# Down projection of a gated feed-forward block by a 2x2 seven-product scheme, with transposed output and sums kept on chip

## The chip, the cores and the metric

One Trainium2 chip, one NeuronCore. The metric is device time in microseconds (us) of one execution. The kernel before was run three times and profiled once.

## The reference

All data are float32. `x` is 2048 tokens by D = 512. Branch A is linear attention with 32 heads of width 16, branch B a bilinear feed-forward block with F = 1792; a sigmoid gate per token mixes them.

```python
g = sigmoid((x * gate_w).sum(-1, keepdims=True))
qkv = x @ wqkv                                   # 512 -> 3*512, 32 heads of 16
phi = lambda t: where(t > 0, t + 1, exp(t)) + 1e-6
kv = einsum("bhsd,bhse->bhde", phi(k), v); z = phi(k) summed over s
a = (phi(q) @ kv / (phi(q) @ z + 1e-6)) @ wo
b = ((x @ w_gate) * (x @ w_up)) @ w_down
out = g * a + (1 - g) * b
```

## The kernel before, in words

Every product of full precision is made of three TensorE matmuls (`mm3`): both operands are split into a high part (rounded to float32r, on ScalarE) and a low part (the difference, on VectorE), and high*high, low*high and high*low are summed in PSUM. TensorE takes a 128x128 block as stationary operand and 512 columns as moving operand.

Stage 1 (up to about 94 us of the profile) computes phi(k) for all tokens and the 512x512 matrix phi(k)^T x (`gt`), the column sums `zacc`, and the gates `gcol` (g) and `ocol` (1-g), one column of 16 token tiles each. `kv_unit` and `wp_unit` then fold the value weights and `wo` into one matrix (`wp`, four blocks of 128 rows) that is applied to phi(q).

Stage 2 goes twice (pair 0, pair 1) over two chunks of 512 tokens (c = 0, 1). A pass has 16 units: 14 "f" units, each 128 columns of `w_gate` and `w_up`, and two "q" units, each 256 columns of the query weights, after f units 5 and 9. A unit computes its 2x2 block product (two chunks by two column blocks) by the Winograd form of Strassen's scheme: seven products, into four PSUM banks Y, X, R, S (`unit`, `product`), each of six matmuls. The weights of a unit come as a load of five blocks (`w_load`), a negated copy of two of them on ScalarE and an accumulating DMA from GpSimd (`w_add`), and are split by `w_high` and `w_low`. The seven combinations of x per pair (`xc`) are parked in DRAM for pair 1 as high and low parts (`xpark`).

The hidden values `hh`, `hl` of two f units are multiplied by two rows of blocks of `w_down` (`dh`, `dl`) in eight jobs of one 128-token tile each (`down_jobs`): stationary are 128 tokens of the hidden values, moving 512 columns of `w_down`, six matmuls a job. A job ends with a scaled accumulation into its tile's sum `acc` by VectorE (`scalar_tensor_tensor` with `ocol`). The phi(q) part goes through the same jobs, with `gcol` and the folded matrix, which lies in DRAM meanwhile (`wpark`) and is loaded again for each q unit. `shares` says how many jobs stand at four places within a unit. Output tiles are tokens by D.

Every engine executes its instructions in the order in which the program writes them. A DMA of the SyncE (SP) queue also waits until the one eight places ahead of it, whose completion semaphore it uses again, has landed.

Of the kernel before, what the change touches and what calls it, by code (L numbers as in the profile page):

```python
# [31 lines left out]
NH = 5  # L32

SLOT = {3: 0, 4: 1, 5: 2, 2: 3, 1: 4, 6: 5, 7: 6}  # L40


@with_exitstack
def gated_mix(ctx: ExitStack, tc, xt, xp, x, wqkv, wq, wq_add, wo, wgu, wgu_add, wdn, gate_w, out):
# [74 lines left out]
    xpark = {i: [dram.tile([P, 2, CH], F32, name=f"xpark{i}{v}") for v in "hl"] for i in range(1, 8)}  # L119
    wpark = [[dram.tile([P, D], F32, name=f"wpark{b}{v}") for v in "hl"] for b in range(KT)]  # L120


    order = []
    for f in range(NF):
        order.append(("f", f))
        if f in (5, 9):
            order.append(("q", f // 9))
# [22 lines left out]
    def w_high(n):  # L150
        if n < len(order):
            wcs[n] = [const.tile([P, 7, 2 * P], F32R, tag=f"wc{v}", name=f"wc{v}", bufs=2) for v in "hl"]
            for a, b in PARTS:
                act(wcs[n][0][:, a:b], raws[n][:, a:b])
# [14 lines left out]
    def x_add(tile_, pair, i, ks):  # L169
# [3 lines left out]
        if one is not None:  # L173
# [3 lines left out]
    accs = [psum.tile([P, D], F32, tag=tag, name=f"gt{d}", bufs=2)  # L177
            for d, tag in enumerate(("att", "att", "dn", "dn"))]
    with tc.tile_pool(name="p1", bufs=2, reuse_waits="tile") as p1:
# [167 lines left out]
        pin(nc.vector.tensor_scalar(ocol, gcol, -1.0, 1.0, op0=ALU.mult, op1=ALU.add))  # L347
        pz = psum.tile([P, D], F32, tag="X", name="pz")
# [11 lines left out]
    jobs, at = [], {}  # L360

    def later(n, place, fn):
        at.setdefault((n, place), []).append(fn)

    def do(n, place):
        for fn in at.pop((n, place), []):
            fn()

    def down(k):
        for fn in jobs[:k]:  # L370
            fn()
        del jobs[:k]

    shares = {2: (0, 1, 1, 1), 6: (1, 0, 1, 0), 7: (1, 0, 1, 0), 10: (1, 1, 1, 2), 11: (1, 2, 1, 2),
              12: (1, 1, 1, 2), 15: (1, 1, 1, 2)}
    early = {units: (2, 3, 1, 2), units + 1: (2, 2, 2, 2)}

    def share(n):
        return early.get(n) or shares.get(n % units, (1, 1, 1, 1))

    def unit(n, quad):

        wh, wl = wcs.pop(n)
        bank = {t: psum.tile([P, CH], F32, tag=t, name=f"b{t}") for t in "YXRS"}

        def reload(i):
            if n + 1 == units:  # L390
                for src, part in zip(xpark[i], xc[i]):
                    dma(part.bitcast(F32), src)

        def product(i, to, start=False):
            for k in range(2):
                ks = slice(k * P, (k + 1) * P)
                mm3(bank[to], (wh[:, SLOT[i], ks], wl[:, SLOT[i], ks]), [v[:, k] for v in xc[i]],
                    start and k == 0, k == 1, not start)
            reload(i)

        m2 = p2.tile([P, CH], F32, tag="t", name="m2")
        cross = p2.tile([P, 2, CH], F32, tag="cross", name="cross")
        product(2, "Y", True)
        act(m2, bank["Y"])
        product(3, "X", True)

        tt(bank["R"], bank["X"], m2, ALU.subtract)
        do(n, "e")
        many = share(n)
        down(many[0])  # L410
        product(4, "Y")
        act(cross[:, 0], bank["Y"])
        do(n, "m")
        do(n, "c")
        down(many[1])
        do(n, "d")
        w_add(n + 2)
        product(1, "R")
        t = p2.tile([P, CH], F32, tag="t", name="t")
        tt(t, bank["R"], cross[:, 0], ALU.add)  # L420
        if n:
            w_high(n + 1)
        do(n, "t")
        product(5, "X")
        tt(bank["S"], t, bank["X"], ALU.subtract)
        act(cross[:, 1], bank["X"])
        if n:
            w_low(n + 1, 0)
        down(many[2])
        if quad:  # L430
            quad(1, 0, cross[:, 0])
        if n:
            w_low(n + 1, 1)
        do(n, "s")
        down(many[3])
        w_low(n + 1, 2)
        w_load(n + 3)
        if quad:
            quad(0, 1, cross[:, 1])
        product(6, "R")  # L440
        if quad:
            quad(1, 1, bank["R"])
        else:
            hh, hl = hidden()
            tt(cross[:, 1], bank["R"], cross[:, 1], ALU.mult)
            act(hh[:, 1], cross[:, 1])
        do(n, "r")
        product(7, "S")
        if quad:
            quad(0, 0, bank["S"])  # L450
        else:
            tt(cross[:, 0], bank["S"], cross[:, 0], ALU.mult)
            act(hh[:, 0], cross[:, 0])

            for c in 1, 0:
                def low(c=c):
                    tt(hl[:, c], cross[:, c], hh[:, c].bitcast(F32), ALU.subtract)

                if n + 1 == len(order):
                    later(n, f"low{c}", low)  # L460
                else:
                    low()
            return hh, hl

    def hidden():
        return [p2.tile([P, 2, CH], F32R, tag=f"h{v}", name=f"h{v}", bufs=NH) for v in "hl"]

    def down_tiles():
        return [p2.tile([P, D], F32R, tag=f"d{v}", name=f"d{v}", bufs=NH) for v in "hl"]

# [3 lines left out]
    def wp_load():  # L474
        att["wv"] = [p2.tile([P, D], F32, tag="acc", name="wv", bufs=8) for _ in range(KT)]
        att["wo"] = [p2.tile([P, D], F32, tag="ph", name="wo_sb", bufs=4) for _ in range(KT)]
        for k in range(KT):
            dma(att["wv"][k], wqkv[k * P:(k + 1) * P, 2 * D:3 * D])
        for k in range(KT):
            dma(att["wo"][k], wo[k * P:(k + 1) * P, :])  # L480

    def g_evac():
        att["g"] = [p2.tile([P, D], F32, tag="acc", name="gts", bufs=8) for _ in range(KT)]
        for d in range(KT):
            if d % 2:
                act(att["g"][d], accs[d])
            else:
                pin(nc.vector.tensor_copy(att["g"][d], accs[d]))

    def kv_unit():  # L490
        pkv = psum.tile([P, KT, P], F32, tag="att", name="pkv", bufs=2)
        for b in range(KT):
            sl = slice(b * P, (b + 1) * P)
            for d in range(KT):
                mm(pkv[:, b], att["wv"][d][:, sl], att["g"][d][:, sl], start=d == 0, stop=d == KT - 1)
        att["pkv"] = pkv

    def kv_split():
        kvm = p2.tile([P, KT, P], F32, tag="z", name="kvm", bufs=4)
        tt(kvm, att["pkv"], bmask[:, None, :].to_broadcast([P, KT, P]), ALU.mult)  # L500
        att["kvm"] = [p2.tile([P, KT, P], F32R, tag="z", name=f"kvm{v}", bufs=4) for v in "hl"]
        split(*att["kvm"], kvm)

    def wo_split(b):
        if b % 2 == 0:
            att.setdefault("woh", []).append(hidden())
        split(*[v[:, b % 2] for v in att["woh"][b // 2]], att["wo"][b])

    def wp_unit(b):
        pw = psum.tile([P, D], F32, tag="att", name="pw", bufs=2)  # L510
        mm3(pw, [v[:, b] for v in att["kvm"]], [v[:, b % 2] for v in att["woh"][b // 2]], True, True)
        d = down_tiles()
        split(*d, pw)
        for there, part in zip(wpark[b], d):
            dma(there, part.bitcast(F32))


    acc = {}

    parts = [(1, 0), (0, 1), (1, 1), (0, 0)]  # L520
    banks = ["dn", "dn"]
    left = {(p, i): NF // 2 + 1 for p in range(NPAIR) for i in range(TPP)}

    def down_jobs(pair, group, col):

        def job(i):
            t = pair * TPP + i
            c, sl = divmod(i, CH // P)
            sl = slice(sl * P, (sl + 1) * P)
            s = col[:, t:t + 1]  # L530
            first = (pair, i) not in acc
            if first:
                acc[pair, i] = p2.tile([P, D], F32, tag="acc", name="acc", bufs=8)
            else:
                left[pair, i] -= 1
            ends = not left[pair, i]

            step = D // 2 if ends and pair and i == TPP // 2 - 1 else D
            for o in range(0, D, step):
                cols = slice(o, o + step)  # L540
                banks.reverse()
                pd = psum.tile([P, D], F32, tag=banks[0], name="pdn", bufs=2)[:, 0:step]
                for j, ((hh, hl), w2) in enumerate(group() if callable(group) else group):
                    mm3(pd, (hh[:, c, sl], hl[:, c, sl]), [v[:, cols] for v in w2], j == 0, j == 1)
# [223 lines left out]
```

## Time and profile before

| | |
|---|---|
| runs (us) | 608.6, 610.45, 611.46; median 610.45 |
| span of the profiled execution | 610.0 us (the page has no other time for it) |
| TensorE matmul | 602.6 us busy, 99% |
| VectorE | 443.7 us, 73% |
| ScalarE | 295.0 us, 48% |
| GpSimd | 46.4 us, 8% |
| DMA | 111.13 MB, mean 182 GB/s |

The busy time of an engine is counted from each instruction's start to its end, and instructions overlap a little; how far apart they start is read from their rows in order of time. "Idle before" is the time for which an engine stood still ahead of the instructions of a group, with what ended it.

### The profile page before, as it was taken

To read this page: it belongs to the slowest core of one execution; us is meant where nothing else is said; L and a number is where in the kernel's file an instruction comes from. 1 tells how busy PE (TensorE), PEld (TensorE's weight loads), DVE (VectorE), ACT (ScalarE), POOL (GpSimd) and SP (SyncE) were. 2 spreads that over 40 slices of the span, in tenths; PEclk is the share of its full clock that TensorE was granted. 3 is DMA by queue.
4 is the path that set the end of the run, shared out by engine and by line. 5 is a ranking of instruction groups with operands and counts; after the bars stand their busy time and mean duration, and the time that the engine had idled before them with its cause. 6 is when DMAs were issued, how large, how long until landed. Compare 5 with 4: busy or idle time off the path is not lost.

```text
span 610.0 us, 7536 instructions
## 1 busy us (share of the span) xinstructions
PE 602.6 (99%) x2657; PEld 495.6 (81%) x2657; DVE 443.7 (73%) x695; ACT 295.0 (48%) x506; POOL 46.4 (8%) x62
## 2 busy tenths in 40 slices
PE   8999999999999999899999999999999999999997
PEld 6888878888888888688888878888888888888886
DVE  6977796666776797777789656456677886668874
ACT  3855665466448453465444332564373354633310
POOL 0011100001111110110100012000000000000000
PEclk9999999999999999899999999999999999999999
DMA  8567956667768977869779966444487455462313
GB/s 295 177 205 138 290 161 167 162 190 224 224 173 205 305 149 227 223 156 262 183 184 316 396 199 188 103 105 103 105 196 193 118 178 142 140 172 52 107 35 139
DMA packets 49703, 111.13 MB, mean 182 GB/s; under 512 B 4737, under 2 KB 13953, under 8 KB 49665
## 3 DMA queue, kind: packets, MB, share of 16 engines
q1 hardware_dynamic: 42112, 82.07, 39.7%
q0 software_dynamic: 7408, 28.32, 25.6%
q8 instruction: 21, 0.34, 0.2%
q10 hardware_dynamic: 144, 0.26, 0.1%
q14 instruction: 18, 0.14, 0.1%
HBM read 92.54 MB, written 18.09 MB: 181 GB/s over the span
## 4 chain that ended last, share of the span: by engine, by line
PE 87%; DMA 9%; DVE 2%; issue 1%; ACT 0%; SPq 0%
PE pdn L52 29%; PE bY L52 13%; PE bR L52 13%; PE bX L52 13%; PE pk L52 7%; PE bS L52 6%; PE gt L52 5%; DMA xc4l<-xpark4l 3%; DMA wr<-in_wgu 3%; DMA dl<-wpark3l 2%; DMA dl<-wpark1l 1%; PE pkv L52 1%; DMA wraw<-in_wqkv 1%; PE pw L52 0%; DVE xnl L61 0%
## 5 line engine op out<-in xcount | busy, mean ns | idle before, releaser
L52 PE MATMUL pdn<-dh,hh 128*128 128x512 f32 x290 | 112.9, 389 | 1.9 <-DMA dh<-wpark1h 1.9
L52 PE MATMUL pdn<-dl,hh 128*128 128x512 f32 x290 | 113.0, 390 | 0.3 <-DMA dl<-wpark1l 0.2
L52 PE MATMUL pdn<-dh,hl 128*128 128x512 f32 x290 | 112.8, 389 | 0.0
L58 ACT ACTIVATE hh<-cross 128x512 fp32r<-128x512 f32 x56 | 35.2, 632 | 99.2 <-DVE cross L61 99.2
L64 DVE SCALAR_TENSOR_TENSOR acc<-pdn,ocol,acc 128x512 f32<-128x512 f32 (+1 forms) x97 | 71.4, 739 | 14.3 <-PE pdn L52 13.1
L61 DVE TENSOR_TENSOR wcl<-wr,wch 128x512 fp32r<-128x512 f32 (+1 forms) x96 | 73.0, 773 | 1.8 <-DMA xpark1l<-cbs 1.2
L52 PEld LDWEIGHTS pdn<-dh,hh 128*128 128x128 f32 x290 | 54.6, 188 | 13.8 <-DMA dh<-wpark1h 2.3
L52 PEld LDWEIGHTS pdn<-dl,hh 128*128 128x128 f32 x290 | 54.6, 188 | 12.5 <-DMA dl<-wpark1l 0.5
L52 PEld LDWEIGHTS pdn<-dh,hl 128*128 128x128 f32 x290 | 54.5, 188 | 11.1
L58 ACT ACTIVATE wch<-wr 128x512 fp32r<-128x512 f32 (+1 forms) x96 | 60.0, 691 | 0.0
L58 ACT ACTIVATE cross<-bY 128x512 f32<-128x512 f32 x32 | 19.1, 598 | 73.3 <-PE bY L52 69.8
L61 DVE TENSOR_TENSOR dl<-wdr,dh 128x512 fp32r<-128x512 f32 x28 | 19.4, 692 | 42.4 <-ACT dh L58 42.4
L52 PE MATMUL bX<-xbl,wch 128*128 128x512 f32 x128 | 49.9, 390 | 0.0
L52 PE MATMUL bX<-xbh,wch 128*128 128x512 f32 x128 | 49.9, 390 | 0.0
L52 PE MATMUL bX<-xbh,wcl 128*128 128x512 f32 x128 | 49.8, 389 | 0.0
L85 POOL DMA_DIRECT2D wr<-in_wgu_add x28 | 24.8, 887 | 275.9 <-DVE dl L61 92.5
L61 DVE TENSOR_TENSOR hl<-cross,hh 128x512 fp32r<-128x512 f32 x56 | 38.0, 688 | 2.7
L58 ACT ACTIVATE cross<-bX 128x512 f32<-128x512 f32 x32 | 19.0, 594 | 31.4 <-DVE bS L61 31.4
L64 DVE SCALAR_TENSOR_TENSOR acc<-pdn,gcol,acc 128x512 f32<-128x512 f32 x32 | 23.8, 750 | 13.7 <-PE pdn L52 13.5
L61 DVE TENSOR_TENSOR bR<-bX,m 128x512 f32<-128x512 f32 x32 | 22.3, 697 | 15.1 <-PE bX L52 15.0
L61 DVE TENSOR_TENSOR bS<-t,bX 128x512 f32<-128x512 f32 x32 | 22.3, 696 | 13.7 <-PE bX L52 13.4
L61 DVE TENSOR_TENSOR t<-bR,cross 128x512 f32<-128x512 f32 x32 | 22.0, 688 | 10.9 <-PE bR L52 10.9
(150 smaller groups left out, 1262.2 us busy)
## 6 DMA issues: line engine op xcount, KB each, us to landing
wr<-in_wgu SPq DMA_DIRECT2D x28, 640.0 KB, 4.2
wr<-in_wgu_add POOLq DMA_DIRECT2D x28, 640.0 KB, 7.9
wdr<-in_wdn SPq DMA_DIRECT2D x28, 256.0 KB, 3.1
xraw<-in_x SPq DMA_DIRECT2D x16, 256.0 KB, 5.2
terms<-zq SPq DMA_DIRECT2D x16, 256.0 KB, 2.3
zt<-terms SPq DMA_DIRECT2D x16, 256.0 KB, 8.3
rb<-den SPq DMA_DIRECT2D x16, 256.0 KB
cbs<-in_xp SPq DMA_DIRECT2D x14, 256.0 KB, 5.7
```

The source lines that it names most:

```text
L52: tc.keep_in_program_order(nc.tensor.matmul(*args, **kw))
L58: pin(nc.scalar.activation(dst, src, func, **kw))
L61: pin(nc.vector.tensor_tensor(dst, a, b, op=op))
L64: pin(nc.vector.scalar_tensor_tensor(dst, a, scalar, b, op0=op0, op1=op1))
L85: tc.keep_in_program_order(nc.gpsimd.dma_start(dst, src, accum_op=ALU.add))
```

## The change

The product with `w_down` is now made by the ordinary Strassen scheme over pairs of f units (`Group`). Its 2x2 blocks are: two units (the contraction), two halves of the 512 output columns, two chunks. Blocks of `w_down` are stationary, hidden values of 512 tokens moving, and so the output is transposed (`out` is D by tokens, turned back on the host). Each of seven products has two jobs (d = 0, 1) of three matmuls. The fourteen product sums per pair (`macc`, the M tiles) stay on chip through six groups: for d = 0 VectorE adds the bank to M, for d = 1 ScalarE puts M into the bank first (`seed`) and copies it back after (`evac`). The seventh group is plain (`plain`, `ends_jobs`): its hidden values are multiplied by a row of 1-g first, the M tiles are combined to four output blocks and scaled by that row, and its jobs also take the phi(q) part, four blocks of contraction, then two.

Five hidden-value combinations per group are formed by VectorE (`total`), seven operands split by `hi_lo`; the weight combinations come as for a unit (`d_load`, `d_add`, `d_high`, `d_low`). The folded matrix `wp` stays on chip. The gates are written to DRAM as `gates` and read back as rows (`omg`) and as `g2`, which is multiplied into the reciprocal of the denominators. The q units come first in each pass. The parked x of pair 1 is one unsplit tile and is split after loading (`x_turn`, `x_split`). 45 tiles of 128x512 are handed out from a list (`get`, `put`). In the words below a slot is one of the seven places of a unit, with one product and, in a group's time, one job; "turn" is the stretch of jobs alone behind the last unit of a pair.

```diff
-    for f in range(NF):
-        order.append(("f", f))
-        if f in (5, 9):
-            order.append(("q", f // 9))
+    order = [("q", j) for j in range(2)] + [("f", f) for f in range(NF)]
...
+        for there, col in zip(gates, (gcol, ocol)):
+            dma(there.rearrange("t p -> p t"), col)
...
+    def d_load(g):
+        if g < NPAIR * NG:
+            draw[g] = p2.tile([P, 7, 2 * P], F32, tag="dr", name="dr")
+            dma(draw[g][:, 0:5], wdn[g % NG])
+
+    def d_add(g):
+        if g < NPAIR * NG and g % NG < NG - 1:
+            act(draw[g][:, 5:7], draw[g][:, 0:2], scale=-1.0)
+            dma_add(draw[g][:, 2:7], wdn_add[g % NG])
...
+        def job(self, i, d):
+            bank = self.banks.pop((i, d), None)
+            seeded = bank is not None
+            if not seeded:
+                bank = job_bank()
+            part, o = DPART[i]
+            w = [v[:, o, d * P:(d + 1) * P] for v in dcs[self.g, part]]
+            mm3(bank, w, self.ops[i], not seeded, True, seeded)
...
+            def evac():
+                if self.first:
+                    macc[i, d] = get("M")
+                    act(f32(macc[i, d]), bank)
+                elif seeded:
+                    act(f32(macc[i, d]), bank)
+                else:
+                    tt(f32(macc[i, d]), f32(macc[i, d]), bank, ALU.add)
...
+    def x_split(i):
+        hi, lo = xc[i]
+        act(hi, lo.bitcast(F32))
+        tt(lo, lo.bitcast(F32), hi.bitcast(F32), ALU.subtract)
...
+    for i, off in zip(UNIT, (36, 38, 40, 41, 42, 43)):
+        tail.setdefault((0, off, "x"), []).append(lambda i=i: x_split(i))
+    later(7 * units + 1, lambda: x_split(7))
...
+    later(0, g2_load)
+    later(9, kv_unit)
...
+    later(0, lambda: d_load(0))
...
+    later(7, lambda: d_add(0))
     wp_load()
```

How many instructions there are (before, after): matmuls of 512 columns 2605, 2539, and of 256 columns 12, 0; VectorE operations on 128x512 606, 703, on 128x768 32, 44, on 128x1024 5, 12; ScalarE activations on 128x512 461, 643, on 128x768 32, 44, on 128x1024 7, 14.

The SP queue at the start of stage 2, before. `wr` are unit weights, `wdr` is a block row of `w_down`, `wv` and `wo_sb` are the value weights and `wo`:

```order
L82 DMA wr<-in_wgu 128x1280
L82 DMA wdr<-in_wdn 128x512
L82 DMA wv<-in_wqkv 128x512 x4
L82 DMA wo_sb<-in_wo 128x512 x4
L82 DMA wdr<-in_wdn 128x512
```

The same place after; `gateg`, `gateo` are the gates in DRAM, `g_982` is `g2`, and `dr` the five blocks of `w_down` of the first group:

```order
L80 DMA wr<-in_wgu 128x1280
L80 DMA gateg<-gcol 128x16x1
L80 DMA gateo<-ocol 128x16x1
L80 DMA wv<-in_wqkv 128x512 x4
L80 DMA wo_sb<-in_wo 128x512 x4
L80 DMA g_982<-gateg 32x1x128 x8
L80 DMA dr<-in_wdn 128x1280
L80 DMA wr<-in_wgu 128x1280
```

The first load for `w_down` moved behind ten more transfers. The third load of `wo` is eight places behind `gateg` and the fourth behind `gateo`, the last of `g2` eight behind that fourth.

ScalarE around the end of the first unit and the start of the second, before (`cross`, `m` are copies of the banks X, Y):

```order
L58 ACTIVATE wr<-wr 128x512
L58 ACTIVATE cross<-bX 128x512
L58 ACTIVATE hh<-cross 128x512 x2
L58 ACTIVATE m_1106<-bY 128x512
L58 ACTIVATE hh<-wo_sb 128x512 x2
```

And after, where the first two units are q units (`ex`, `phq` are exp and relu of a bank):

```order
L56 ACTIVATE ex<-bS 128x512
L56 ACTIVATE phq<-bS 128x512
L56 ACTIVATE dr<-dr 128x512
L56 ACTIVATE m_1118<-bY 128x512
L56 ACTIVATE zq<-phq,ezcol,zcol 128x512 x2
L56 ACTIVATE wr<-wr 128x512
L56 ACTIVATE c_1159<-bY 128x512
```

The negated copy of the first `dr` now stands right ahead of the copy of bank Y that the second unit's third product, into the same bank, has to wait for.

VectorE at the change of pairs, before: from the last unit of pair 0 the work of the next unit follows at once.

```order
L61 TENSOR_TENSOR cross<-bS,cross 128x512
L61 TENSOR_TENSOR hl<-cross,hh 128x512 x2
L61 TENSOR_TENSOR zt<-zt 128x512
L61 TENSOR_TENSOR zt<-zt 128x256
L64 SCALAR_TENSOR_TENSOR den<-zt 128x128
L61 TENSOR_TENSOR bR<-bX,m_2819 128x512
```

After, the last rows of the turn and the first of pair 1's first unit:

```order
L59 TENSOR_TENSOR ol<-phq,oh 128x512 x3
L59 TENSOR_TENSOR xal<-xal,xah 128x1024
L59 TENSOR_TENSOR xbl<-xbl,xbh 128x1024
L59 TENSOR_TENSOR M<-M,pdn 128x512
L59 TENSOR_TENSOR xc4l<-xc4l,xc4h 128x1024
L59 TENSOR_TENSOR xc1l<-xc1l,xc1h 128x1024
L59 TENSOR_TENSOR xbl<-xbl,xbh 128x1024
L59 TENSOR_TENSOR xc6l<-xc6l,xc6h 128x1024
L59 TENSOR_TENSOR M<-M,pdn 128x512
L59 TENSOR_TENSOR xal<-xal,xah 128x1024
L59 TENSOR_TENSOR bR<-bX,m_3381 128x512
```

The combination of banks X and Y into R (`bR`) now stands behind the low halves of seven x tiles and, further up, behind the combination of the M tiles.

More of the change, by code (lines that the diff above doesn't have):

```diff
@@ L379, in gated_mix, with get @@
[L379 to L384, printed above, removed]
-        wh, wl = wcs.pop(n)
[L387 to L392, printed above, removed]
+    spare, held = list(range(NW)), {}
+    def get(name):
+        k = spare.pop(0)
+        w = p2.tile([P, CH], F32R, tag=f"w{k}", name=name)
+        held[id(w)] = (k, w)
+        return w
@@ L415, in unit @@
[L415 to L433, printed above, removed]
```

667 lines of the change are left out of this document (432 added, 235 removed).

## The prediction, made before the changed kernel was run

> **What bounds the kernel now.** I read the page's busy shares first, then its chain, then the idle time of the groups by line, then rows in order of time at the places that the change touches.
>
> ```profile
> span 610.0 us, 7536 instructions
> PE 602.6 (99%) x2657; PEld 495.6 (81%) x2657; DVE 443.7 (73%) x695; ACT 295.0 (48%) x506; POOL 46.4 (8%) x62
> PE 87%; DMA 9%; DVE 2%; issue 1%; ACT 0%; SPq 0%
> L52 PE MATMUL pdn<-dh,hh 128*128 128x512 f32 x290 | 112.9, 389 | 1.9 <-DMA dh<-wpark1h 1.9
> ```
>
> TensorE works for 99% of the span, and the chain that ended last is 87% its own. The costliest group has one idle stretch worth naming, 1.9 us for the folded matrix from DRAM. So time is saved by fewer matmuls and by that stall, and lost wherever TensorE is made to wait anew. The 389 ns of a matmul is its length; how far apart they start is read from the chain, in which twelve stand in one row (start, length).
>
> ```profile
> 19.24 2.72 PE gt L52 x12
> 21.96 2.72 PE pk L52 x12
> ```
>
> 2.72/12 = 0.2267 us is the price of one 512-wide matmul. A unit's slot (six) is 1.36 us, a job of the new scheme (three) 0.68, a slot with a job 2.04.
>
> **A, the matmuls.** Per pair the new jobs issue 6 Strassen groups x 42, a plain group's 48 and 96 for phi(q): 396, where 432 stood (at 512 columns). The totals fall by 66 of 512 columns, and the 12 of 256 columns at the very end go too.
>
> ```profile
> 604.96 0.28 PE L52 MATMUL pdn<-dh,hh 128*128 128x256 f32 x1
> 606.27 0.28 PE L52 MATMUL pdn<-dh,hl 128*128 128x256 f32 x1
> 606.59 0.48 DVE L64 SCALAR_TENSOR_TENSOR acc<-pdn,ocol,acc 128x256 f32<-128x256 f32 x1 [0.23 <-PE pdn L52]
> ```
>
> First and last of the twelve are 1.31 us apart, 0.119 each. 66 x 0.2267 + 12 x 0.119 = 15.0 + 1.4: **-16.4**. The end now has an ordinary bank to add instead of a half one (0.69 us, rows below, for 0.48) and a whole tile to write: **+0.3**.
>
> **B, the folded matrix stays on chip.** Rows around the stall (start, length, idle before), and the window behind it (the 0.50 is the granted clock):
>
> ```profile
> 251.96 0.39 PE L52 MATMUL pdn<-dh,hl 128*128 128x512 f32 x1
> 254.25 0.49 PE L52 MATMUL pdn<-dh,hh 128*128 128x512 f32 x1 [1.91 <-DMA dh<-wpark1h]
> ...
> 258.37 0.49 PE L52 MATMUL pdn<-dh,hh 128*128 128x512 f32 x1
> 256.00:258.00 2.00, 2.00 (x7) 1.51 (x6) 0.75 (x1) 0.00 (x0) 0.87 (x1) 0.50 0.12 25
> ```
>
> From 251.96 to 258.37 eleven intervals took 6.41 us, not 11 x 0.2267 = 2.49. 3.9 us were lost, 1.9 to 2.0 of them after the wait, at a granted clock of 0.50. No DMA stands there any more: **-3.9**. The same rows price any new stall of about 2 us: its length and 1.9 more.
>
> **What VectorE and ScalarE must now do beside it.** Start-to-start times, by rows that follow each other without idle time:
>
> ```profile
> 80.05 0.68 DVE L64 SCALAR_TENSOR_TENSOR zacc<-ph,zacc 128x512 f32<-128x512 f32 x1
> 80.65 1.22 DVE L61 TENSOR_TENSOR xal<-cbs,xah 128x1024 fp32r<-128x1024 f32 x1
> 81.78 0.95 DVE L61 TENSOR_TENSOR wcl<-wr,wch 128x768 fp32r<-128x768 f32 x1
> 82.65 0.69 DVE L64 SCALAR_TENSOR_TENSOR ph<-e,r 128x512 f32<-128x512 f32 x1
> 308.17 0.62 ACT L58 ACTIVATE dh<-wdr 128x512 fp32r<-128x512 f32 x1
> 308.69 0.62 ACT L58 ACTIVATE cbh<-cbs 128x512 fp32r<-128x512 f32 x1
> ```
>
> VectorE: 0.60 us for 512 columns, 1.13 for 1024, 0.87 for 768. ScalarE: 0.52 for 512, and I allow it 0.52 x 768/512 = 0.78 for 768. A group's time is two units, 14 slots with a job, 28.56 us of TensorE. VectorE has 35 operations of 512 and 3 of 768 in it, 23.6 us; ScalarE 36 and 3, 21.1 us. Both fit, so the splits, totals, seeds and bank additions of groups 1 to 5 cost nothing: TensorE's jobs hide them, with 5 us to spare. If that cover goes, each us over is a us of waiting (rival 3). The accumulations of `d_add` are issued from GpSimd in place of others, and its busy share of 8% hides their issue.
>
> **D, the change of pairs.** Behind pair 0's last unit TensorE has 30 jobs, 20.4 us. In it VectorE has 31 operations of 0.60 (M tiles combined and scaled, phi(q) split, banks added) and six low halves of x at 1.13: 25.4 us, with 1.1 carried in. Then come another bank, another half of x, and `bR`: 25.4 + 1.1 + 0.6 + 1.13 + 0.6 = 28.8 us. TensorE needs `bR` for the fourth product of pair 1, at 20.4 + 3 x 2.04 = 26.5. 2.3 late, with a semaphore's latency **+2.5**. Before, VectorE had only a unit's usual work there. The ends are 0 (the engine ran ahead into the turn) and 5.9 (if operations start as far apart as they last: 0.69 and 1.22).
>
> **E, first group of a pair.** Before its jobs a unit's slots are 1.36 us short, and the group's seven operands fall due. In slots 134 to 137 (counted seven to a unit) VectorE has fifteen operations, 11 x 0.60 + 2 x 0.87 + 0.6 for two narrow ones = 8.9 us, against 3 x 1.36 + 2.04 = 6.1: 2.8 late, where one slot of 2.04 can be lost before a product waits: 0.8 and latency, +1.0. The same at pair 0's slots 24 and 25 comes to +0.7, and the chain kvm to kvl at slot 11 to +0.4. **+2.1**, ends 0 and 4.
>
> **F, the start of stage 2.** Here the change moves a chain of DMAs ahead of work of TensorE. Rows of before:
>
> ```profile
> 91.91 0.17 DVE L347 TENSOR_SCALAR ocol<-gcol 128x16 f32<-128x16 f32 x1
> 93.81 0.47 PE L52 MATMUL bY<-xah,wch 128*128 128x512 f32 x1
> 94.73 1.75 SPq L82 DMA_DIRECT2D wo_sb<-in_wo  x4
> wo_sb<-in_wo SPq DMA_DIRECT2D x4, 256.0 KB, 4.0
> wr<-in_wgu SPq DMA_DIRECT2D x28, 640.0 KB, 4.2
> ```
>
> ScalarE executes the negated copy `dr<-dr` ahead of `m2` of the second unit, and TensorE's tenth product, due at 93.81 + 9 x 1.36 = 106.05, waits for that. `dr` must have landed by 106.05 - 0.52 - 0.52 - 0.1 = 104.9. On SP, `dr` stands behind two gate writes, eight loads, eight reads of `g2`; the last `g2` waits until the last `wo` has landed, that one until `gateo` has. The last `wo` landed at about 94.73 + 1.31 + 4.0 = 100.1; a step of the queue is 0.4 (1.75/4). Undisturbed, `dr` lands at 100.1 + 0.4 + 0.4 + 4.2 = 105.1, 0.2 late. The writes delay it: 2 x 2048 separate elements of 4 bytes, 256 for each of 16 engines, in front of the loads: 0.256 us for each ns that one takes, and 0.7 for the loads that wait for them. Nothing like it was in the kernel. Nearest are these windows (packets, share of 16 engines):
>
> ```profile
> DMA packets 2, 0.00 MB, mean 0 GB/s; under 512 B 2, under 2 KB 2, under 8 KB 2
> q1 hardware_dynamic: 2, 0.00, 0.2%
> q0 software_dynamic: 16, 0.00, 4.8%
> DMA packets 1087, 1.04 MB, mean 259 GB/s; under 512 B 32, under 2 KB 979, under 8 KB 1087
> q1 hardware_dynamic: 1087, 1.04, 79.0%
> ```
>
> Two tiny packets in 0.5 us (120.0 to 120.5) held 0.2% of 16 engines: 8 ns each. Sixteen of GpSimd's (117.0 to 117.5, third row) held 4.8%: 24 ns. The terms, mostly 512-byte writes (272 to 276), 79% of 4 us: 46.5 ns. I take 16 ns, a tiny packet's read and write, since size is what these elements share with it: 0.2 + 0.7 + 4.1 = 5.0 us of stall and 1.9 of slow clock, **+6.9**. The ends are 0.2 (hidden) and 46.5 ns: 0.9 + 11.9 + 1.9 = 14.7. While TensorE waits there, the accumulating DMAs of the first units have time to land, so I add nothing for them.
>
> The Trainium skill, "DMA: Bandwidth & Descriptors", section "Rules for kernel authors", says that a strided last dimension lowers to one descriptor per element; its section "Bandwidth" has about 10.5 ns per packet. By that price F would be about 5.5 us and the sum about 600.5, an estimate; no run here shows such a write yet.
>
> **Sum.** 610.0 - 16.4 + 0.3 - 3.9 + 2.5 + 2.1 + 6.9 = 601.5. The profiled execution is 0.45 under the median of the runs, so 602 against 610.45. About 0.5% (607.4 to 613.5) is what can be told from no change.
>
> **Rivals.**
>
> 1. The gates are hidden, F is 0.2: 595. For it: tiny packets of 8 ns; the eight loads of before had all landed by 100. Against it: even at 8 ns the sum of F is 0.9 + 2.0. Price 594.5 to 597.
>
> 2. Gate writes as dear as the terms' (46.5 ns): F = 14.7, 609.5; at 62 ns, 0.9 + 15.9 + 1.9 = 18.7 and 613.5, from which it is slower. For it: the only DRAM writes of small rows in the trace cost that. Against it: they carry 512 bytes, and their share includes waiting for data. 607 to 616. The same page's "Specifications" say that under 512 bytes an engine reads, modifies and writes; this trace has no such write, and the rule would put e towards this rival.
>
> 3. VectorE becomes the bound, and the kernel slower. Row for it:
>
> ```profile
> DVE dl L61 <- ACT dh L58: 44.4, 30, 3.1
> ```
>
> VectorE waited 30 times, 44.4 us together, for high halves of ScalarE; the new groups have ten such pairs of high and low each, in both orders, with only 5 us to spare. If operations start 0.69 and 0.95 apart, a group is 27.0 of 28.56, and waits of more than 1.6 us in a group stall TensorE. D's late start becomes 5.9, 3.6 more than summed, and with x us lost in each of 12 groups the time is 602 + 3.6 + 12x: slower from x = 0.7, 607 to 616 for x from 0.1 to 0.9. Against it: the 0.60 is read from rows without idle time, and in those 30 waits TensorE did not stand still.
>
> That the scheme doesn't take matmuls away is excluded by the counts of the instructions.
>
> **Chances.** Forecast as summed (597 to 607): 0.50. Rival 1: 0.20. Rival 2: 0.17, of it 0.01 still faster, 0.09 the same, 0.07 slower. Rival 3: 0.13, 0.08 the same, 0.05 slower. Faster 0.50 + 0.20 + 0.01 = 0.71, same 0.17, slower 0.12. The range, 594.5 to 611, leaves out the upper parts of rivals 2 and 3 (together about 0.16) and some 0.03 under a clean start.
>
> **What would show it.** A: matmuls into `pdn` down, TensorE busy near 586 us. B: no `wpark`, no granted clock of 0.5 near the first phi(q) jobs. D: an idle stretch of about 2 us before a `bR` product, released by VectorE, about 6 us into pair 1. E: idle time under 1 us in the second unit of the first group. F: a gap near 106 us whose chain goes to ScalarE's `m2`, `dr` and its DMA, with packets of 4 bytes on the queue; its length over 0.9 gives the price of one. Wrong would be: gaps in every group on `hl` or on M tiles (rival 3), VectorE busy far over 443.7 + 87 us (97 more of 512 at 0.69, 12 of 768 at 0.95, 7 of 1024 at 1.22), or a stall of another load behind the SP queue that I have not seen.

## The result, and the profile after

The changed kernel takes 642.1 us (641.6 to 644.6) where the one before takes 611.0: ratio 1.052, interval 1.048 to 1.056. It is slower by 31 us; the forecast was 602, range 594.5 to 611.

The page of the changed kernel, its span, busy shares, chain, and two groups (x count | busy, mean ns | idle before):

```profile
span 642.8 us, 7716 instructions
PE 596.3 (93%) x2579; PEld 483.4 (75%) x2579; DVE 507.0 (79%) x813; ACT 398.2 (62%) x707; POOL 57.0 (9%) x74
PE 64%; DMA 17%; DVE 12%; ACT 3%; issue 3%; SPq 0%; DVEq 0%; ACTq 0%; POOL 0%; POOLq 0%
L50 PE MATMUL pdn<-hh,dh 128*128 128x512 f32 x200 | 78.4, 392 | 4.4 <-ACT pdn L56 4.4
L50 PE MATMUL bY<-xc4h,wch 128*128 128x512 f32 x64 | 26.4, 412 | 22.2 <-ACT m L56 22.2
```

The chain was 87% TensorE's before and is 64% now; DMA has 17% and VectorE 12%. One group alone waits 22.2 us.

To place the rest I add up lost time: for each matmul row, its distance to the next one less the pitch, the usual distance (0.2267 us for 512 columns, in proportion for fewer). About 2.5 us of it in every kernel is not waiting: the 40 narrow products start further apart than their width says. Times are those of the profiled executions, and the last column is the median of the timed runs.

| kernel | to 92 us | units of pair 0 | first turn, `bR` | units of pair 1 | last turn | sum | time |
|---|---|---|---|---|---|---|---|
| before | 3.1 | 7.4 | 0.9 | 0.0 | 0.0 | 11.4 | 611.0 |
| changed | 2.3 | 43.7 | 7.4 | 4.3 | 2.4 | 60.1 | 642.1 |

Matmul time at the pitch fell by 16.3 us (66 x 0.2267 and 12 x 0.113); lost time rose by 48.7; the tail, from the last matmul to the end, is 0.5 longer. 48.7 + 0.5 - 16.3 = 32.9, and the spans differ by 32.8. So the scheme did save its matmuls, and three times as much went into waiting.

The largest piece, in the chain (start, length), on SP, on ScalarE and on TensorE; the window is the one right behind the gap (granted clock 0.50):

```profile
91.12 20.66 DMA gateo<-ocol
111.80 9.72 DMA wo_sb<-in_wo
122.17 4.23 DMA dr<-in_wdn
```

```profile
91.12 0.88 SPq L80 DMA_DIRECT2D gateo<-ocol  x1
95.85 16.27 SPq L80 DMA_DIRECT2D wo_sb<-in_wo  x4
112.18 9.95 SPq L80 DMA_DIRECT2D g<-gateg  x8
122.17 0.41 SPq L80 DMA_DIRECT2D dr<-in_wdn  x1
126.42 0.63 ACT L56 ACTIVATE dr<-dr 128x512 f32<-128x512 f32 x1 [21.46 <-DMA dr<-in_wdn]
126.96 0.58 ACT L56 ACTIVATE m<-bY 128x512 f32<-128x512 f32 x1
127.59 0.79 PE L50 MATMUL bY<-xc4h,wch 128*128 128x512 f32 x1 [21.78 <-ACT m L56]
```

```profile
127.59:131.00 3.41, 3.41 (x10) 2.83 (x11) 0.68 (x1) 2.32 (x4) 1.49 (x2) 0.50 0.63 90
```

This is the chain that the prediction named: gate writes, the last `wo`, `g2`, `dr`, the negated copy, `m2`, TensorE. It cost 21.8 us and about 2 of slow clock: the granted clock stayed at 0.50 until 131.6 us, so that six matmuls of 512 columns started 0.43 to 0.60 us apart. Smaller gaps follow, each with the wait of ScalarE or VectorE that made it:

```profile
140.66 0.50 PE L50 MATMUL bS<-xah,wch 128*128 128x512 f32 x1 [1.93 <-DVE bS L59]
172.72 0.63 ACT L56 ACTIVATE dr<-dr 128x512 f32<-128x512 f32 x1 [5.48 <-DMA dr<-in_wdn]
174.38 0.50 PE L50 MATMUL pdn<-woh,kvh 128*128 128x512 f32 x1 [2.46 <-ACT M L56]
215.18 0.63 ACT L56 ACTIVATE wr<-wr 128x512 f32<-128x512 f32 x1 [4.12 <-DMA wr<-in_wgu]
216.35 0.50 PE L50 MATMUL pdn<-hh,dh 128*128 128x512 f32 x1 [3.11 <-ACT pdn L56]
356.44 0.50 PE L50 MATMUL pdn<-hl,dh 128*128 128x512 f32 x1 [1.66 <-DVE hl L59]
371.58 0.50 PE L50 MATMUL pdn<-ol,wph 128*128 128x512 f32 x1 [1.89 <-DVE ol L59]
383.74 0.50 PE L50 MATMUL bR<-xc1h,wch 128*128 128x512 f32 x1 [1.34 <-DVE bR L59]
608.75 0.50 PE L50 MATMUL pdn<-hl,dh 128*128 128x512 f32 x1 [1.06 <-DVE hl L59]
```

At 174 and 216 us it is a negated copy on ScalarE that waits for its load, with bank copies and seeds behind it. At 140 us it is VectorE, which has the split of the masked kv matrix ahead of `bS`; in the turns (345 to 385, 600 to 625) it is VectorE too.

The first turn has a waiting copy as well (ScalarE, then VectorE):

```profile
358.21 0.63 ACT L56 ACTIVATE dr<-dr 128x512 f32<-128x512 f32 x1 [4.24 <-DMA dr<-in_wdn]
359.40 0.69 DVE L59 TENSOR_TENSOR hl<-c,hh 128x512 fp32r<-128x512 f32 x1 [1.81 <-ACT hh L56]
```

ScalarE's `hh` stands behind that copy, so VectorE stood still for 1.81 us; from there it works without a pause until `ol` (the low half of phi(q)), which TensorE gets 1.89 us late at 371.58.

### The profile page after: what moved, and what is told of

Read it like the earlier page. It is cut to its first block, busy times and chain, and to the rows that moved or that the text cites. A ratio compares the mean times of both kernels' runs of the same rounds, so it can differ in the third digit from the quotient of the medians.

```text
span 642.8 us, 7716 instructions
## 1 busy us (share of the span) xinstructions
PE 596.3 (93%) x2579; PEld 483.4 (75%) x2579; DVE 507.0 (79%) x813; ACT 398.2 (62%) x707; POOL 57.0 (9%) x74
## 4 chain that ended last, share of the span: by engine, by line
PE 64%; DMA 17%; DVE 12%; ACT 3%; issue 3%; SPq 0%; DVEq 0%; ACTq 0%; POOL 0%; POOLq 0%
PE pdn L50 18%; PE bY L50 10%; PE bR L50 9%; PE bX L50 8%; PE pk L50 7%; PE gt L50 6%; PE bS L50 5%; DMA dr<-in_wdn 5%; DVE M L59 4%; DMA wr<-in_wgu 4%; DMA gateo<-ocol 3%; DMA xw<-in_xp 2%; DMA wo_sb<-in_wo 2%; DMA wr<-in_wgu_add 1%; DVE wcl L59 1%
## 5 line engine op out<-in xcount | busy, mean ns | idle before, releaser
L56 ACT ACTIVATE M<-pdn 128x512 f32<-128x512 f32 x98 | 58.6, 598 | 38.4 <-PE pdn L50 35.6
L50 PE MATMUL pdn<-hh,dh 128*128 128x512 f32 x200 | 78.4, 392 | 4.4 <-ACT pdn L56 4.4
L50 PE MATMUL pdn<-hl,dh 128*128 128x512 f32 x200 | 78.5, 393 | 3.6 <-DVE hl L59 3.6
L59 DVE TENSOR_TENSOR M<-M,pdn 128x512 f32<-128x512 f32 x86 | 58.9, 685 | 26.5 <-PE pdn L50 26.4
L50 PE MATMUL pdn<-hh,dl 128*128 128x512 f32 x200 | 78.3, 392 | 0.0
L50 PEld LDWEIGHTS pdn<-hh,dh 128*128 128x128 f32 x200 | 37.7, 188 | 13.4 <-ACT pdn L56 5.6
L50 PEld LDWEIGHTS pdn<-hl,dh 128*128 128x128 f32 x200 | 37.8, 189 | 12.5 <-DVE hl L59 4.8
L50 PE MATMUL bY<-xc4h,wch 128*128 128x512 f32 x64 | 26.4, 412 | 22.2 <-ACT m L56 22.2
L50 PEld LDWEIGHTS pdn<-hh,dl 128*128 128x128 f32 x200 | 37.7, 188 | 7.8
L56 ACT ACTIVATE pdn<-M 128x512 f32<-128x512 f32 x70 | 41.7, 596 | 0.0
L59 DVE TENSOR_TENSOR hl<-c,hh 128x512 fp32r<-128x512 f32 x56 | 38.4, 686 | 2.5 <-ACT hh L56 2.4
L56 ACT ACTIVATE c<-bX 128x512 f32<-128x512 f32 x28 | 16.8, 598 | 28.2 <-DVE bS L59 26.8
```

Source lines behind the costliest of these rows:

```text
L50: tc.keep_in_program_order(nc.tensor.matmul(*args, **kw))
L56: pin(nc.scalar.activation(dst, src, func, **kw))
L59: pin(nc.vector.tensor_tensor(dst, a, b, op=op))
```

## The experiments

All timed runs (ratio to the kernel before on the same chip, 95% interval) and the lost time of their profiles. e10 to e13 are the same program up to the last unit of pair 0, and their 13.9 to 15.5 us in pair 0 show how far one execution differs from another:

| kernel | time | ratio | pair 0 | first turn | pair 1 | last turn |
|---|---|---|---|---|---|---|
| e1 gates as rows | 629.4 | 1.033 (1.029-1.037) | 28.2 | 6.6 | 5.3 | 2.4 |
| e2 `dr` copy late | 640.4 | 1.051 (1.047-1.055) | 38.3 | 6.2 | 4.4 | 2.4 |
| e3 gates behind | 636.3 | 1.044 (1.041-1.047) | 35.2 | 7.2 | 4.6 | 2.4 |
| e4 one element write | 635.9 | 1.043 (1.039-1.048) | 33.4 | 6.2 | 4.1 | 2.4 |
| e5 = e1, `dr` before `wo` | 626.0 | 1.027 (1.021-1.034) | 23.8 | 7.0 | 4.8 | 2.4 |
| e6 = e5, kv split late | 625.2 | 1.026 (1.018-1.034) | 24.4 | 7.2 | 4.6 | 2.4 |
| e7 = e6, copies late | 624.0 | 1.022 (1.016-1.028) | 23.4 | 6.2 | 5.2 | 2.4 |
| e8 = e6, negations late | 617.1 | 1.012 (1.009-1.016) | 18.3 | 5.5 | 2.4 | 2.3 |
| e9 = e6, no M sums | 617.9 | 1.015 (1.011-1.019) | 23.0 | 1.8 | 4.9 | 0.3 |
| e10 combined, seeded turn | 618.6 | 1.015 (1.011-1.018) | 15.5 | 9.8 | 2.3 | 2.4 |
| e11 = e10, GpSimd | 625.9 | 1.027 (1.024-1.029) | 15.5 | 16.7 | 2.3 | 2.4 |
| e12 combined, no seeds | 613.0 | 1.006 (1.003-1.009) | 13.9 | 5.5 | 2.7 | 2.4 |
| e13 = e12, turn order | 616.1 | 1.011 (1.007-1.015) | 14.2 | 8.1 | 2.3 | 2.8 |
| e14 = e13, z chain | 615.7 | 1.011 (1.008-1.014) | 11.2 | 10.9 | 2.8 | 2.8 |
| e15 = e12, z chain, `bR` | 607.9 | 1.000 (0.998-1.002) | 15.4 | 4.4 | 1.8 | 2.3 |
| e16 = e15, order, negation | 610.3 | 1.003 (1.001-1.005) | 11.8 | 4.7 | 5.8 | 2.6 |

**The gate writes (e1 to e4).** e1:

```diff
-            dma(there.rearrange("t p -> p t"), col)
+        mm(pz[0:2 * NT, P:2 * P], goc, ident, start=True, stop=True)   # goc: gcol, ocol
+        pin(nc.vector.tensor_copy(grow, pz[0:2 * NT, P:2 * P]))
+        for i in range(2):
+            dma(gates[i], grow[i * NT:(i + 1) * NT])
```

> The gates are turned by one small TensorE product with a unit matrix and written as rows of 512 bytes; the order of the SP queue stays. Theory W (the 4096 separate 4-byte writes are the price, about 80 ns each per engine): the stall at the second unit's third product falls from 21.8 us to 2 or less, the slow clock behind it goes, and the time falls by 20 to 25 us, to 617 to 622. Rival O (the queue's order, eight places ahead, is the price, whatever the writes are): dr still lands after 115 and the time stays above 630.

12.7 us went, half of what W said. Both theories hold a part. The rows of e1 (SP, ScalarE, TensorE):

```profile
99.11 9.23 SPq L80 DMA_DIRECT2D g<-gateg  x8
108.39 0.41 SPq L80 DMA_DIRECT2D dr<-in_wdn  x1
112.20 0.63 ACT L56 ACTIVATE dr<-dr 128x512 f32<-128x512 f32 x1 [6.76 <-DMA dr<-in_wdn]
113.36 0.80 PE L50 MATMUL bY<-xc4h,wch 128*128 128x512 f32 x1 [7.09 <-ACT m L56]
```

14.7 us of the stall was the element writes; 7.1 stays, because `dr` is issued only at 108.4, behind the reads of `g2`. What SP waited for longest there (us in total, times, longest) is a load of `wv`:

```profile
SPq L80 <- DMA wv<-in_wqkv: 3.7, 1, 3.7
```

The fourth read of `g2` uses the semaphore of the last `wv`, issued at 96.3, and went out only at 104.9. After the fifth, at 105.9, the reads and `dr` follow each other by 0.63 us.

e4 writes `gates[0]` as a row and `gates[1]` by elements:

> As the first, but one of the two gates is still written as 2048 elements of 4 bytes. Theory W, 0.256 us for each ns halves to 0.128: the stall is 10 to 12 us and the time lies half way, 629 to 633. Rival (a fixed cost of the first such write, or of the order): nearer to 642 or to 619 than to the middle.

```profile
121.78 0.80 PE L50 MATMUL bY<-xc4h,wch 128*128 128x512 f32 x1 [14.97 <-ACT m L56]
```

With no, one and two element writes the stall is 7.1, 15.0, 21.8 us: nearly even steps, so W's dose, on top of the 7.1 that it did not count on (stall and time lie 3 us above its forecast). 14.7 us for 256 elements per engine is 57 ns each.

e2 only moves the copy, e3 only the writes:

```diff
-    later(7, lambda: d_add(0))
+    later(12, lambda: d_add(0))
```

> Only the negated copy of the first dr and its accumulating load move five slots later; the 4-byte writes stay. If TensorE stands still at 106 us only because ScalarE waits for dr ahead of the copy of bank Y, then that gap goes, and the next thing behind the same writes shows: the value weights wv, queued right behind them, for the kvm product at slot 9, landing near 116. A gap of 8 to 10 us at about 108 instead of 21.8 at 106, time 628 to 634. If the writes held more than this chain, the gap stays above 18 us.

```diff
+    later(2, gates_out)          # the two writes, taken from the end of stage 1
-    later(0, g2_load)
+    later(16, g2_load)
```

> The two 4-byte gate writes move behind the loads of wv, wo, dr and into the third slot, the reads of g2 to the seventeenth. Theory W (price is in the packets, wherever they stand): wv, wo and dr land by 103, but the writes still hold the queue for 20 us, and the unit weights wr, loaded behind them, come about 13 us late for ScalarE's negated copy: a gap of 10 to 16 us, time 628 to 636. Rival O (price is in the place on the queue): no gap over 2 us, time 617 to 622.

In e2 the long gap is gone and TensorE waits for `wv` near 108 us as said (3.7 us, where 8 to 10 were said), but another 7.3 us before an R product at 130, behind a negated copy that waited 21 us for `wr`, brings nearly all back: 640.4, a miss of 6. In e3 ScalarE waits 13 us for the next unit weights instead (TensorE 8.3 and, at 165, 7.6), and the time is at the upper end of W's forecast:

```profile
111.59 0.38 PE L50 MATMUL pkv<-gts,wv 128*128 128x128 f32 x1 [3.73 <-DMA wv<-in_wqkv]
120.18 0.63 ACT L56 ACTIVATE wr<-wr 128x512 f32<-128x512 f32 x1 [13.05 <-DMA wr<-in_wgu]
```

The first row is e2's, the second e3's. The writes hold whatever is loaded behind them, wherever they stand.

**Queue and VectorE order at the start (e5, e6).**

```diff
+        d_load(0)                                    # e5: between wv and wo
         for k in range(KT):
             dma(f32(att["wo"][k]), wo[k * P:(k + 1) * P, :])
...
-    later(0, g2_load)
+    later(14, g2_load)
-    later(11, kv_split)                              # e6
+    later(13, kv_split)
...
-    later(0, lambda: d_load(0))                      # e5
```

> On top of the gates written as rows: the first dr goes ahead of wo on the SP queue and the eight reads of g2 go fourteen slots later. Theory O (of the 7.1 us that stayed with rows, the queue was the cause: dr was issued at 108.4 behind the reads of g2, which waited for the last wo): dr lands near 104, the gap at 113 us falls to under 1 us, and with its slow clock 8 to 9 us go: 620 to 622. Rival (the accumulating load of the third unit's weights, which shares the engines, sets the landing, wherever dr stands): dr still lands after 109, gap of 4 us or more, time 626 or more.

> As the one before, and the split of the masked kv matrix (kvm, kvl) two slots later. Theory V (on VectorE kvm and then kvl, which waits for ScalarE's kvh, stand ahead of the combination bS that TensorE needs): the gap of 1.9 us before a bS product near 126 us and the slow clock behind it go, 3.5 to 4 us less than the one before. Rival: VectorE is short there anyway (wcl and phq stand there too), the gap comes back one or two products later, under 1.5 us less.

e5: the gap fell from 7.1 to 1.5 us, but the time by 3.5 only, and a gap at 158 grew from 1.4 to 5.7. `dr` landed neither near 104 (O) nor after 109 (the rival); ScalarE still waited for it:

```profile
107.54 0.63 ACT L56 ACTIVATE dr<-dr 128x512 f32<-128x512 f32 x1 [1.20 <-DMA dr<-in_wdn]
```

Issued at 97.8, beside `wv`, `wo` and the accumulating load (97.2 to 107.3), `dr` took 9.8 us to land; in e1, issued at 108.4 when these had landed, it took 3.8. So place and company both count. e6: the `bS` gap went, a wait for `m` before the next unit grew to 2.0, 0.8 us less: its rival held.

**Volume or place of the copies (e7, e8).** In e6 ScalarE waits twice for loads, and TensorE for it:

```profile
146.85 0.63 ACT L56 ACTIVATE wr<-wr 128x512 f32<-128x512 f32 x1 [7.36 <-DMA wr<-in_wgu]
156.16 0.63 ACT L56 ACTIVATE dr<-dr 128x512 f32<-128x512 f32 x1 [7.19 <-DMA dr<-in_wdn]
157.81 0.79 PE L50 MATMUL pdn<-woh,kvh 128*128 128x512 f32 x1 [6.46 <-ACT M L56]
```

```diff
-        later(20, lambda i=i: dma(xpark[i], xp[1, SUMS[i][1]]))     # e7
+        later(62, lambda i=i: dma(xpark[i], xp[1, SUMS[i][1]]))
-                when(12, lambda: d_add(g + 1))                      # e8
+                when(15, lambda: d_add(g + 1))
-        if s == (1 if kind == "q" else 3):                          # e8, w_add
+        if s == (1 if kind == "q" else 4):
```

> On top of the kv split two slots later: only the two copies of parked x from DRAM to DRAM (0.5 MB each, read and written) move from slot 20 to slot 62. Theory B (the transfers of the first units fill the DMA engines, and ScalarE's negated copies wait for loads that come late): the two waits of 7.2 to 7.4 us of ScalarE for wr and dr before 157 us shrink by 2 to 4 us each, the gap of 6.5 us near 158 falls to 0 to 3, time 4 to 8 us less. Rival P (not the volume but the place of the copies in ScalarE's order): gap within 1.5 us of what it was.

> On the same base: ScalarE's negated copy of dr stands three slots later and that of wr in an f unit one slot later, with their accumulating loads. Theory P (copies that stand in ScalarE's order before their load has landed block seeds, bank copies and m2): the gaps near 158 (6.5 us) and near 195 (3.0) fall below 2 and 1 us, time 6 to 10 us less. Theory B (volume): the gaps stay or turn up at the high halves, which then wait for the accumulating loads: under 3 us less.

e7: the gap at 158 fell to 1.4 us, as theory B said, but lost time ahead of the turn fell by 1.0 and the time by 1.2 (its four runs lie between 617.8 and 625.3): the waits moved. e8: 8.1 us less; the gaps near 158 and 195 are gone, as P said, though one at 143 grew from 0.7 to 1.9 and one of 2.6 opened at 165. The place of the copies, with the accumulating loads that moved along, counts more than the volume.

**The turns (e9 to e16).** e9 skips the `tt` of the twelve sums in `ends`.

> On the same base: the twelve sums of M tiles in each of the two turns are left out, 7.2 us of VectorE work in each (they change the output). Theory T (VectorE is the bound from the last unit on, so that everything behind it is late by the work that stands ahead): the gaps of TensorE at 352 to 354 and before bR of the next pair, about 4 us with the rests, go, those at 331 and 338, which stand ahead, stay; with the second turn's 0.8 us, 4 to 5.5 us less. Rival (each gap is a latency of one chain, ScalarE's high half then VectorE's low half): under 1.5 us less.

7.3 us less, more than T's 4 to 5.5. First turn from 7.2 to 1.8 us, last from 2.4 to 0.3; even the gap ahead of them shrank, because two sums stand before the `hl` that it waits for:

```profile
334.60 0.50 PE L50 MATMUL pdn<-hl,dh 128*128 128x512 f32 x1 [0.43 <-DVE hl L59]
```

Two ways of giving work of VectorE to other engines:

```diff
+                        if seeded:                       # e10: six of eight banks
+                            act(box["bank"], f32(c_tile(d, c)))
...
+            if seeded:
+                act(f32(w), bank)
-        tt(lo, lo.bitcast(F32), hi.bitcast(F32), ALU.subtract)     # e11: x_split
+        pin(nc.gpsimd.tensor_tensor(lo, lo.bitcast(F32), hi.bitcast(F32), op=ALU.subtract))
```

> The later negations (617.1) with the other finds put together: the two DRAM copies at slot 62, the first dr's negation at slot 11, the kv split at slot 12, the split of wo a slot later, and in the turns six of the eight banks seeded with their scaled tile by ScalarE and copied back by it, which takes 3.6 us from VectorE in each turn. If the reasons found add up: the gaps at 108 and 124 (1.8 + 2.1 and slow clock 1.7) go, those of the turns fall from 7.8 to about 4.5, together 6 to 9 us less: 608 to 611, no slower than the kernel before. If each relief only moves the wait: 613 or more.

> The same with the seven low halves of pair 1's x subtracted by GpSimd, which takes 7.9 us from VectorE at the change of pairs. Theory T: the gap before bR (1.5 us with its rest) goes, and what is left of the turn's gaps shrinks: 1 to 3 us less than the one before. Rival: GpSimd needs over 3 us for each 1024 columns, or slows VectorE while it works; then TensorE waits for xc parts in pair 1's first unit, and the time is the same or up to 5 us longer.

> The combined kernel (618.6) without the seeded banks of the turns; the other four edits stay. Theory S (ahead of the turns the finds do add up, 1.8 us less lost by 190 us than with the later negations alone; it was the seeds, which stand in ScalarE's order just ahead of the product that needs them, that lost 4.3 us more in the turns): the gaps ahead of products with seeded banks (0.8, 1.3, 1.3, 2.7 us) go, those of VectorE come back, 3 to 5 us less: 613.5 to 615.5. Rival: the four edits themselves cost the turns something, and the time stays within 1.5 us of 618.6.

e10 took 618.6 us, not 608 to 611. The four edits at the start helped, but did not add up in full: the gaps at 108 and 124 went (5.6 us with their slow clock), others came behind them, and lost time in pair 0 fell from 18.3 to 15.5 (13.9 in e12). The seeds took more than they gave: e12 without them is 5.6 us faster, a little over S's 3 to 5. e10's longest such gap, GpSimd's group in e11, and one row of VectorE in e11:

```profile
375.70 0.50 PE L50 MATMUL pdn<-oh,wph 128*128 128x512 f32 x1 [2.55 <-ACT pdn L56]
L707 POOL TENSOR_TENSOR xbl<-xbl,xbh 128x1024 fp32r<-128x1024 f32 x2 | 4.8, 2410 | 0.0
356.76 5.40 DVE L62 SCALAR_TENSOR_TENSOR phq<-ex,phq 128x512 f32<-128x512 f32 x1
```

e11 is 7.2 us slower. GpSimd takes 2.41 us for 1024 columns, where VectorE needs 1.22, but no gap of TensorE waits for a low half. The row shows what happened: one operation of VectorE, 0.68 us in e10, lasted 5.40, while GpSimd subtracted (from 356.3, then from 359.2 to 361.6). `bS` and what ScalarE makes of it came late, and TensorE waited 5.69 us at 366.5. So the trace shows the second half of the rival: VectorE was held up while GpSimd worked.

e13 to e16 keep VectorE's work and move it:

```diff
+            some = 0 if k < 3 else 2 if k < 8 else 1                # M sums later: e13, e14, e16
-    later(7 * units + 1, lambda: x_split(7))
+    later(7 * units + 3, lambda: x_split(7))                        # all four
-        for k, s in enumerate((0, 2, 4, 5)):
+        for k, s in enumerate((0, 2, 5, 6)):                        # phi(q) splits: e13, e14
-        for e, s in zip((1, 2, 3), (23, 24, 25)):
+        for e, s in zip((1, 2, 3), (25, 26, 27)):                   # z chain, other steps alike: e14 to e16
-            when(14, lambda: d_add(g + 1))
+            when(24, lambda: d_add(g + 1))                          # e16
```

> On the combined kernel without seeds (613.0): the same VectorE work in the turns in another order. The sums and scalings of M tiles start three jobs later, behind the low halves hl that the next jobs need; the last two splits of phi(q) stand behind bS in the last unit; the low half of the seventh x part stands behind bR. Theory Q (what TensorE waits for there is the order on VectorE, not the amount of its work): the gaps at 320, 327, 353 and 576 us (0.9, 1.8, 1.5, 1.2) fall to 0.3 or less each, 4 to 5.5 us less: 607.5 to 609. Theory T (amount): the work moved turns up as gaps later in the same turn, or before the next pair's products: less than 2 us less.

> The one before, and the denominators' chain of both q units two slots later (loads zt, sums, reciprocal, reads rb), the scaling of phi(q) three. Theory Q: the wait of VectorE for rb at 160 us no longer stands ahead of bS, the gap of 2.1 us near 163 and the slow clock behind it fall below 0.7, and the three gaps of 0.6 at 390 to 399 lose the zt sums ahead of them: 2.5 to 4.5 us less than the one before, 604 to 606. Rival: rb and zt come late by the DMA engines whatever the slot, and the gap moves with them: within 1.5 us of the one before.

> The combined kernel without seeds (613.0), with the denominators' chain two slots later (as in the run where it took 3.3 us of lost time away ahead of the turn) and the low half of the seventh x part behind bR, and the turn's sums left where they were. If both effects add up: lost time 3 us less ahead of the turn, 1.5 less at bR: 607.5 to 610, level with the kernel before. If the turn gives it back again: 612 or more.

> The one before, with the M sums three jobs later again and the negated copy of the next pair's first dr ten jobs later. Theory N (with the sums moved, VectorE stood still for 3.2 us at 325 us only because ScalarE waited for dr ahead of the high half hh; so it is again a copy ahead of its load): VectorE works through, the gap of 4.7 us at 343 stays below 1.5, those at 327 and 576 below 0.5, 1.5 to 3 us less than the one before. Theory T (amount of VectorE work): 1.8 us of gap come back at ol, within 1 us of the one before.

e13: the four gaps fell to 0.5 or less, nearly as Q said, but one of 4.5 us opened at `ol` in the first turn and one of 1.5 in the last. The time rose by 3.0 instead of falling by 4 to 5.5. The rows at the longer one, TensorE and ScalarE:

```profile
343.15 0.79 PE L50 MATMUL pdn<-ol,wph 128*128 128x512 f32 x1 [4.50 <-DVE ol L59]
327.38 0.63 ACT L56 ACTIVATE dr<-dr 128x512 f32<-128x512 f32 x1 [3.87 <-DMA dr<-in_wdn]
```

e14: ahead of the turn 3.0 us less lost, the gap before `bS` near 163 gone, as Q said for the z chain; the turn gave it back (the copy of `dr` waited 5.8 us, the gap at `ol` is 6.4), and 615.7 lies far from the 604 to 606 of Q. e15 joins what had helped and leaves the turn's sums: 607.9, level with the kernel before (its twelve runs lie between 606.3 and 613.8). That is 5.1 us less than e12, but e12 ran on another chip, and the ratios differ by 0.6% only, which is 3.8 us. Its profiled execution took 611.0 and has a new gap of 2.1 us at 185, so that the table doesn't show which edit gave the gain. e16: the copy no longer waits, VectorE works almost without a pause from 319 to 340 us, and the gap at `ol` is 1.5 instead of the 4.5 of e13. So N accounts for most of that gap, and the rest is VectorE's work ahead of `ol`; as e16 differs from e13 in the z chain and the phi(q) splits too, the shares are not exact. The first turn as a whole lost 4.7, not less than the 4.4 of e15. In pair 1 VectorE waited 3.2 us for `rb` (the reciprocals read back), and e16 is 2.4 us slower than e15: neither N's gain nor T's level.

## Why the prediction was wrong, point by point

The sum had lost time rise by 7.6 us (6.9 + 2.5 + 2.1 - 3.9); it rose by 48.7.

**A, held.** 16.3 us of matmul time were saved (16.4 forecast). The sign given for it, TensorE busy near 586 us, did not come (596.3), in part because busy time counts a matmul at the slow clock as longer (0.63 us at 177.4, 0.40 at 179.7). **B, held**: no slow stretch stands at the phi(q) jobs, and no folded matrix is loaded. Between 251.96 and 258.37 stand ten intervals, not eleven, so the stall was worth 4.1 us. Its price for any stall of about 2 us, "its length and 1.9 more", held at 140.66 (1.93 us), but not at 371.58, where the clock stayed at full speed after 1.89. **The tail** grew by 0.5, not 0.3.

**F, the place right, the size wrong by 17 us.** Forecast 6.9, measured 21.8 + 2.0. Two steps failed.

"I take 16 ns, a tiny packet's read and write". The packets' own records are near that, in the changed kernel's windows from 91 to 101 and from 101 to 112.2:

```profile
DMA packets 4123, 0.05 MB, mean 5 GB/s; under 512 B 4105, under 2 KB 4105, under 8 KB 4123
q1 hardware_dynamic: 4123, 0.05, 45.7%
DMA packets 312, 0.54 MB, mean 48 GB/s; under 512 B 53, under 2 KB 53, under 8 KB 311
q1 hardware_dynamic: 311, 0.53, 90.0%
```

45.7% of 16 engines for 10 us over 4123 packets is 17.7 ns each. But they landed 20.7 us after issue, and for eleven more microseconds the loads behind them moved at 48 GB/s. The price was not in a packet's record but in what followed it. By e1 and e4 the writes cost 14.7 us of stall, e = 57 in place of 16: above the 46.5 that I took as the upper end, and within rival 2, whose mechanism was right. Its chance of 0.17 rested on a bound from 512-byte writes. The other 7.1 us stand where the formula has 0.9, which is the second step.

The Trainium skill, "DMA: Bandwidth & Descriptors", section "Specifications", has it that an engine reads, modifies and writes below 512 bytes. Rows of 512 bytes took the 14.7 us away, which agrees with the rule; no run shows the reading itself, or tells it from the sheer number of packets (4096 against 32 rows). By the about 10.5 ns per packet that the Trainium skill has in section "Bandwidth" of the same page F would have been 5.5, an estimate; the packets' records show 17.7, the stalls 57.

"Undisturbed, `dr` lands at 105.1": with rows it landed at 112.2. The sum let the queue go on when the last `wo` had landed, at 100.1, in steps of 0.4. In e1 the last `wv` held it until 104.9, a `wo` until 105.9, and a read of `g2` took 0.63. The accumulating load of the third unit's weights ran beside, from 96.3 to 105.7; in the trace of before it was issued at 100.2, about when the last `wo` landed. "I add nothing for them" is the step that looks wrong: beside that load and `wv` and `wo`, `dr` took 9.8 us (e5) instead of 3.8. But no run leaves the accumulating load alone out, so its share is not shown.

**The cover of groups 1 to 5, wrong.** "Both fit, so [they] cost nothing" compared amounts of work per 28.56 us. ScalarE had room, but executes in order, and it now carries seeds and bank copies behind negated copies that wait for loads. In the changed kernel that cost 5.3 us (at 174 to 181) and 5.0 (at 216), slow clock included, 1.2 more at 472, and the wait in the first turn; e8, which moves only these copies and their accumulating loads, gained 8.1. The prediction used just this wait for the first copy, in F, but not for the later ones; it was not among the rivals, and only the last sign, "a stall of another load", comes near it.

**D and E, too small.** Forecast for VectorE at the change of pairs 2.5, first groups and kv chain 2.1, last turn 0. Measured: first turn 7.4 (0.9 before), kv chain 3.8 with slow clock instead of 0.4, pair 1 4.3 instead of 1.0 (with the 1.2 at 472, which are ScalarE's), last turn 2.4. The late `bR` was there (1.5, not 2.5); what I left out is that TensorE waits earlier in the turn too, for `hl` and `ol`, which stand behind M sums, and for `ol` also because of the waiting copy. e9 shows the amount: 7.2 us of work left out of each turn took 5.4 and 2.1 us of waiting away. So rival 3 (VectorE the bound) holds in the turns, and not in the groups between, where lost time was zero from 220 to 345 us but for 0.6.

What it came to: 16 us saved, and after the repairs that the runs point to (e15) still 15 us more lost time than before. That is why the best version is level and not faster. Open is how much of the rest is VectorE's amount and how much its order: leaving work out helped (e9), of the ways of moving it only the one at `bR` seems to have (first turn 5.5 to 4.4, within what executions differ by, though its gap of 1.4 is gone).

## What to carry to other kernels

An operation that waits for a load costs what stands behind it on its engine, so ask of each copy on a shared engine whether its load has landed by then, and move it later before moving the load. A write of separate 4-byte elements to DRAM must be priced by when it lands and by what is loaded behind it; turn it on chip into rows. Work given to an idle engine can hold up a busy one: look at the lengths of the busy engine's operations too. A total of busy time under 80% is no cover by itself: sum it for the stretches where the new work is concentrated, from the last unit to the first product of the next pass.

## What the runs showed of the hardware

The second of two writes of 2048 elements of 4 bytes landed 20.7 us after its issue, although each packet's record lasts 17.7 ns only, and the loads behind them moved at 48 GB/s. GpSimd needed 2.41 us for a subtraction of 128x1024 floats, VectorE 1.22; while GpSimd worked, an operation of VectorE that takes 0.68 lasted 5.40 (e11).

After the wait of 21.8 us the granted clock was 0.50 for 4.0 us more, after that of 1.93 us (at 140.66) for 3.4: the loss behind them was 1.7 to 2 us. It does not follow every gap. In all traces together each gap of TensorE of 3.1 us or more was followed by it; of those of 1.8 to 3.0 us, 18 were and 11 were not.
